# A fused attention and two mixtures on one core: the first unit's ScalarE and VectorE in source order, weight blocks in fixed places, and later token transfers

## The chip, the core and the metric

One NeuronCore of a Trainium2 chip runs the whole kernel as one program. The metric is the device time in microseconds; less is better. TensorE does the matmuls, VectorE, ScalarE and GpSimd the elementwise work, SyncE issues nearly all transfers.

## What is computed

Causal attention over 4 batches, 8 heads, 576 positions, head size 64, with a bias from a running sum of max(s, 0); then two mixtures of 2304 tokens, width 512, inner width 2048.

```
scores = q @ k.T / 8 + min(-(cum[i] - cum[j]), 0), causal;  attn = softmax(scores);  x = attn @ v
x = (h * sigmoid(1.702 h)) @ w_out          with h = x @ w_in        (first mixture)
out = (s * relu(h)**2 + b) @ w_out2         with h = x @ w_in2       (second mixture)
```

The four weight matrices reach the kernel as 64-bit floats. A block of 128 rows or columns is 512 KB.

## The kernel before

**Units.** Attention and first mixture go over eight units: first the first 320 positions of each batch (units 0 to 3), then the other 256 (units 4 to 7). While the mixture of unit u runs on TensorE, the attention of unit u + 1 is put between its matmuls (`run`). Unit 0's attention has no mixture beside it: it runs alone, in ten steps. Step s does the scores (`qk`, three chunks of 64, 128 and 128 rows) of head s, `pv` of head s - 2, and the transposes of head s - 1, in that order on TensorE. Unit 0's matmuls take plain float32 operands; all others take operands split into an upper and a lower part (hi and lo, `split_x`, `split_w`).

**A head on the other engines.** Each chunk's scores are reduced by VectorE (L283) out of one of two PSUM buffers (psS), then ScalarE takes exp (L289). Behind the last chunk VectorE makes tot and its reciprocal (L293, L294), ScalarE normalises the last chunk (L111) and GpSimd the others (L113). ScalarE copies the transposes (L319) and the result of pv (L350). For every second head a token part is split (L390 on ScalarE, L391 on VectorE).

**Weights.** A block is fetched (`fetch_w`, L125), joined from its 64-bit halves (`join_w`: L139 on ScalarE; L140 and L141 on VectorE) and split (`split_w`: the upper part by L149 on ScalarE, the lower by L150 on VectorE). The sixteen blocks of the first layer (wi) are loaded during unit 0's attention, up to two a step from step 1, and wait for their join in tiles with the tag "wo", of which there are sixteen. The sixteen of the second layer (wo) are loaded in `run(0)`, through three tiles tagged "pair".

**Order.** The tile framework plans the order of every engine's instructions by its own costs. Within `manual_schedule(engines=...)` the engines named keep the source's order; instructions from elsewhere can still be put between. Before, the whole kernel names TensorE, unit 0's attention TensorE and SyncE, and the last unit's mixture with the second mixture's first block of tokens TensorE, ScalarE and VectorE.

**The last unit and the second mixture.** `first_whole` runs unit 7's mixture alone: 16 blocks h (12 matmuls each), and from the fifth step on the output of the block four earlier. The second mixture's weights go through nine tiles: `fetch_to`, `join_next`, `split_next`, a join in every step between a block's th (L426) and its g (L430). `second` then runs the second mixture on 512 tokens at a time; its tokens come back from DRAM (`fetch_x`, L538) and are split (`parts_x`, L544 on ScalarE, L545 on GpSimd).

Of the kernel before, what the change touches and what calls it, by code (L numbers as in the profile page):

```python
# [11 lines left out]
F32R = mybir.dt.float32r  # L12
# [26 lines left out]
def f32(ap):  # L39
    return ap.bitcast(F32)  # L40
# [27 lines left out]
def fused_kernel(ctx: ExitStack, tc: tile.TileContext, qkT, vP, s, w1i, w1o, w2i, w2o, s2, b2, out):  # L68
# [59 lines left out]
    def join_w(came):  # L128
# [3 lines left out]
        else:  # L132
# [10 lines left out]
            )  # L143
            return f32(lower)

    def split_w(single, tag, f):

        w = wp.tile([P, 2, CM], F32R, tag=tag, name=f"{tag}{f}")
        nc.scalar.activation(w[:, 0, :], single, AF.Copy)  # L149
        nc.vector.tensor_tensor(w[:, 1, :], single, f32(w[:, 0, :]), ALU.subtract)  # L150
        return w

    def load_w(stage, src, tag, f):
        return split_w(join_w(fetch_w(stage, src, f)), tag, f)
# [2 lines left out]
    with ExitStack() as p1:  # L157
# [15 lines left out]
        def setup():  # L173
# [6 lines left out]
            prep_to(0)  # L180
# [41 lines left out]
        def prep(n):  # L222
            u, h = units[n // H], n % H
            J, nj = u.i1, len(u.keys)
            raw = tile([size["n"] + size["keys"]], "raw")

            r = u.b * H + h
            qc, kc = (slice(0, u.n), slice(u.n, u.n + J)) if u.half == 0 else (slice(J, J + u.n), slice(0, J))
            src = qkT[u.b, h, :, : u.n + J] if u.half == 0 else qkT[u.b, h, :, u.i0 :]
            heads[n] = t = {"x": {}, "qc": qc, "kc": kc}  # L230

            def beside(to):
                nc.sync.dma_start(to[D:R, kc], rows_d[0, r, :, :J])
                nc.sync.dma_start(to[D:R, qc], rows_d[1, r, :, u.i0 : u.i1])

            if n < H:
                nc.sync.dma_start(raw[:D, : u.n + J], src[:D])
                if n > 0:
                    beside(raw)
            else:  # L240
                nc.sync.dma_start(raw[:, : u.n + J], src)
            if h % 2 == 0:
                vraw = tile([size["blocks"], P], "vraw")
                nc.sync.dma_start(vraw[:, :nj, :], vP[u.b, h // 2, :, :nj, :])
                vs[n] = vs[n + 1] = vraw
            if n < H:
                t["parts"] = [(raw, R)]
                return


            hi = tile([size["n"] + size["keys"]], "hi", F32R)
            lo = tile([size["n"] + size["keys"]], "lo", F32R)
            beside(f32(lo))
            scaled(nc.scalar if n < 2 * H else nc.vector, hi[:, : u.n + J], raw[:, : u.n + J])
            nc.sync.dma_start(f32(lo[:D, qc]), f32(hi[:D, qc]))
            nc.vector.tensor_tensor(hi[D:, qc], raw[D:, qc], f32(hi[D:, qc]), ALU.subtract)
            nc.gpsimd.tensor_tensor(lo[:D, kc], raw[:D, kc], f32(hi[:D, kc]), ALU.subtract)  # L257
            t["parts"] = [(lo, R), (hi, P)]
            if h % 2 == 0:
                v = tile([size["blocks"], 4, D], "v", F32R)  # L260
# [5 lines left out]
        def qk(n, c):  # L266
            u, t = units[n // H], heads[n]
            a0, a1 = u.chunks[c]
            w = a1 - a0
# [20 lines left out]
            last = len(u.chunks) - 1  # L290
            if c < last:
                return
            nc.vector.tensor_scalar(out=tot[:, : c + 1], in0=tot[:, : c + 1], scalar1=1e-9, scalar2=None, op0=ALU.add)  # L293
            nc.vector.reciprocal(tot[:, : c + 1], tot[:, : c + 1])  # L294
            for k, (b0, b1) in enumerate(u.chunks):
# [73 lines left out]
        n_prep = [0]  # L369

        def prep_to(n):
            while n_prep[0] <= min(n, limit - 1):
                prep(n_prep[0])
                n_prep[0] += 1

        def attend(item):
# [118 lines left out]

        with tc.tile_pool(name="half0", bufs=1) as pool, tc.manual_schedule(engines={PE}):
            attention_pool(pool, B * H, 0)
            x0 = []
            with tc.manual_schedule(engines={PE, SP}):
                setup()  # L500
                for step in range(H + 2):
                    for item in attention_items(step):
                        if item[2] == H - 1 and item[1] == "pv":
                            x0 += [split_x(0, cc) for cc in range(NC - 1)]
                            for f in range(3):
                                h_begin(0, f, x0)
                        if item[2] < H:
                            attend(item)
                    for f in range(len(wi), min(NF, 2 * step)):
                        wi[f] = load_w((wp, "wo", NF), w1i, "wi", f)  # L510
                    if step == 1:
                        nc.sync.dma_start(s_sb, s2.partition_broadcast(P))
                        nc.sync.dma_start(b_sb, b2.partition_broadcast(P))

            def load_wo(f):
                wo[f] = load_w((pool, "pair", 3), w1o, "wo", f)

            run(0, x0)
            for ui in range(1, B - 1):
                run(ui, [])  # L520


        with tc.tile_pool(name="half1", bufs=1) as pool, tc.manual_schedule(engines={PE}):
            attention_pool(pool, 2 * B * H, 1)
            prep_to(B * H)
            for ui in range(B - 1, len(units) - 1):
                run(ui, [])

# [37 lines left out]
    def first_whole(ui):  # L566
# [2 lines left out]
        py = [psY.tile([P, 512], F32, tag="y", name="py3") for _ in range(NC)]  # L569
        for f in range(NF + LEAD):  # L570
            if f < NF:
                for _ in h_item(ui, f, x, join_next):
                    pass
            else:
                join_next()
# [68 lines left out]
            fetch_to(k + 1 + FETCHED)  # L644

    with tc.manual_schedule(engines={PE}):
        xs = [parts_x(fetch_x(*blocks[0], cc), blocks[0][1]) for cc in range(NC)]
        with tc.manual_schedule(engines={PE, ACT, DVE}):
            fetch_to(FETCHED)
            for f in first_whole(len(units) - 1):  # L650
                split_next()
            later, raws = [], []
            for f in second(*blocks[0], xs, False):
                split_next()
                if f in (NF - 5, NF - 1):
                    later += [parts_x(raw, blocks[1][1]) for raw in raws]
                if f in (NF - 9, NF - 5):
                    raws = [fetch_x(*blocks[1], len(later) + cc) for cc in range(2)]
# [48 lines left out]
```

## Time and profile before

| | |
|---|---|
| time, median of 3 runs | 1061.58 us (1060.53 to 1063.24) |
| profiled execution: time, span | 1062.38 us, 1060.6 us |
| TensorE busy (share of the span) | 1016.2 us (96%) |
| VectorE, ScalarE, GpSimd busy | 647.3 us (61%), 535.9 us (51%), 346.5 us (33%) |
| TensorE's waits from 112 to 600 us, all | 11.6 us, the longest 1.5 us |
| one weight block on VectorE (L140, L141, L150, medians up to 112 us) | 0.43, 0.69, 0.68 us |
| a step of the second mixture (760.61 to 766.04 us) | 5.4 us |
| a split of 512 tokens' columns (L544 on ScalarE, L545 on GpSimd) | 0.63, 1.27 us |

The span is the profiled part of the execution. PE is TensorE, PEld its weight loads, DVE VectorE, ACT ScalarE, POOL GpSimd, SP SyncE. "L141" is line 141 of the kernel before. Matmuls overlap their successors, so a group's time is best read from its start to the next group's start.

### The profile page before, as it was taken

The page shows a single profiled execution, that of the slowest core. Times are in us where ns is not written, and L with a number is a line of the kernel's source. Part 1 is how long each engine was busy: PE and PEld are TensorE (multiplying, and loading weights), DVE is VectorE, ACT ScalarE, POOL GpSimd, SP SyncE. Part 2 cuts the span into 40 slices and gives each one's busy share as a digit, 9 for nine tenths or more (in the row PEclk, how much of TensorE's full clock was granted, in tenths as well). Part 3 has the DMA queues.
Part 4 walks back from the last instruction along what each step waited for, and adds up shares of the span by engine and source line. Part 5 has one row for each costly group of instructions (what it writes and reads, how often), then busy time and mean ns, then how long its engine had stood idle before and what let it go on. Part 6 is the DMA issues. An engine that isn't in the chain of part 4 may idle for free.

```text
span 1060.6 us, 17331 instructions
## 1 busy us (share of the span) xinstructions
PE 1016.2 (96%) x6216; PEld 909.3 (86%) x6216; DVE 647.3 (61%) x1441; ACT 535.9 (51%) x1252; POOL 346.5 (33%) x382
## 2 busy tenths in 40 slices
PE   5988999999999999999999989999999999999998
PEld 3458989999989999999999989888788888888887
DVE  4689877567467788878887579864323323232343
ACT  4788856656536646656656567543322322222222
POOL 1115535335335435445445243112410210111011
PEclk9999999999999999999999999999999999999999
DMA  5665332221042232222221176510300100100010
GB/s 180 195 237 184 124 97 61 62 82 44 8 130 75 63 99 70 83 91 72 87 85 51 38 252 209 178 61 21 109 1 0 65 1 1 45 1 1 1 40 21
DMA packets 39181, 85.51 MB, mean 81 GB/s; under 512 B 5660, under 2 KB 16536, under 8 KB 39096
## 3 DMA queue, kind: packets, MB, share of 16 engines
q1 hardware_dynamic: 38888, 84.27, 25.5%
q8 instruction: 49, 0.80, 0.3%
q14 instruction: 36, 0.29, 0.1%
q10 hardware_dynamic: 208, 0.13, 0.0%
HBM read 70.29 MB, written 10.03 MB: 76 GB/s over the span
## 4 chain that ended last, share of the span: by engine, by line
PE 77%; DVE 10%; DMA 4%; ACT 3%; issue 3%; POOL 1%; SPq 1%; DVEq 0%; ACTq 0%; POOLq 0%
PE py L604 17%; PE ph L554 17%; PE py L444 14%; PE ph L404 13%; PE ps L277 5%; PE pst L315 4%; PE po L342 3%; DVE hi L115 3%; PE py L580 2%; DVE x L283 1%; DMA pair<-w1i 1%; PE po L336 1%; ACT x L289 1%; DVE pair L141 1%; DMA pair<-w1o 1%
## 5 line engine op out<-in xcount | busy, mean ns | idle before, releaser
L404 PE MATMUL ph<-xT,wi 128*128 128x320 f32 (+1 forms) x1536 | 246.6, 305 | 10.9 <-DVE th L426 7.2
L404 PEld LDWEIGHTS ph<-xT,wi 128*128 128x128 f32 x1536 | 217.2, 193 | 12.9 <-DVE th L426 7.8
L444 PE MATMUL py<-g,wo 128*128 128x320 f32 (+1 forms) x1344 | 215.1, 304 | 0.0
L604 PE MATMUL py<-wo,g 128*128 128x512 f32 x864 | 208.2, 390 | 1.9 <-POOL g L563 1.8
L554 PE MATMUL ph<-xT,wi 128*128 128x512 f32 (+1 forms) x960 | 208.4, 368 | 0.0
L554 PEld LDWEIGHTS ph<-xT,wi 128*128 128x128 f32 x960 | 169.0, 188 | 31.0
L604 PEld LDWEIGHTS py<-wo,g 128*128 128x128 f32 x864 | 161.1, 188 | 35.9 <-POOL g L563 2.9
L444 PEld LDWEIGHTS py<-g,wo 128*128 128x128 f32 x1344 | 187.9, 189 | 0.8
L558 DVE TENSOR_TENSOR r<-r 128x512 f32<-128x512 f32 (+1 forms) x80 | 53.1, 664 | 195.7 <-ACT r L557 195.7
L431 POOL TENSOR_TENSOR g<-th,g 128x320 fp32r<-128x320 f32 (+1 forms) x128 | 117.3, 917 | 117.5 <-ACT g L430 117.2
L563 POOL TENSOR_TENSOR g<-r,g 128x512 fp32r<-128x512 f32 (+1 forms) x40 | 48.9, 1222 | 308.6 <-PE py L604 167.5
L289 ACT ACTIVATE x<-x,m 64x64 f32<-64x64 f32 (+2 forms) x160 | 89.5, 560 | 100.1 <-DVE m L283 98.5
L557 ACT ACTIVATE r<-ph 128x512 f32<-128x512 f32 (+1 forms) x80 | 44.4, 555 | 152.0 <-PE ph L554 150.4
L257 POOL TENSOR_TENSOR lo<-raw,hi 64x576 fp32r<-64x576 f32 (+1 forms) x56 | 68.3, 1220 | 122.3 <-issue 57.1
L283 DVE CUSTOM_DVE_ANT_0 x<-ps,mask 64x64 f32<-64x64 f32 (+2 forms) x160 | 68.0, 426 | 52.3 <-PE ps L277 50.5
L315 PE MATMUL pst<-ident,x 128*128 128x128 f32 (+2 forms) x480 | 85.8, 287 | 10.0 <-DVE ph L324 8.1
L562 ACT ACTIVATE g<-r 128x512 fp32r<-128x512 f32 (+1 forms) x80 | 47.1, 589 | 93.0 <-DVE r L559 93.0
L113 POOL TENSOR_SCALAR x<-x,tot 64x64 f32<-64x64 f32 (+1 forms) x96 | 47.6, 503 | 94.1 <-DVE tot L294 66.4
L321 ACT ACTIVATE ph<-pst 64x256 fp32r<-64x256 f32 (+2 forms) x144 | 67.0, 473 | 20.7 <-PE pst L315 19.2
L315 PEld LDWEIGHTS pst<-ident,x 128*128 128x128 f32 (+2 forms) x480 | 54.7, 136 | 24.9 <-DVE ph L324 13.0
L430 ACT ACTIVATE g<-th 128x320 fp32r<-128x320 f32 (+1 forms) x128 | 56.3, 440 | 35.6 <-DVE th L426 35.0
L115 DVE TENSOR_SCALAR hi<-raw 128x832 fp32r<-128x832 f32 (+1 forms) x48 | 69.2, 1441 | 2.3 <-DMA raw<-qkT 2.2
(71 smaller groups left out, 1314.2 us busy)
## 6 DMA issues: line engine op xcount, KB each, us to landing
raw<-qkT SPq DMA_DIRECT2D x32, 416.0 KB
pair<-w1o SPq DMA_DIRECT2D x16, 512.0 KB
pair<-w1i SPq DMA_DIRECT2D x16, 512.0 KB
pair<-w2i SPq DMA_DIRECT2D x16, 512.0 KB
pair<-w2o SPq DMA_DIRECT2D x16, 512.0 KB
raw<-qkT SPq DMA_DIRECT2D x24, 320.0 KB
vraw<-vP SPq DMA_DIRECT2D x16, 320.0 KB
out<-y SPq DMA_DIRECT2D x17, 256.0 KB
```

What stands on the lines that cost most here:

```text
L115: nc.vector.tensor_scalar(out=out, in0=in_, scalar1=scale, scalar2=None, op0=ALU.mult)
L257: nc.gpsimd.tensor_tensor(lo[:D, kc], raw[:D, kc], f32(hi[:D, kc]), ALU.subtract)
L283: nc.vector.tensor_tensor_reduce(out=x[:w, j0:j1], in0=ps[:w, : j1 - j0], in1=mask[:w, WIDE - a0 + j0 : WIDE - a0 + j1], scale=-1.0 / ROOT ...
L289: nc.scalar.activation(x[:w, :a1], x[:w, :a1], AF.Exp, bias=least, scale=-1.0, accum_out=tot[:w, c : c + 1])
L315: nc.tensor.transpose(ps[: j1 - j0, at : at + a1 - a0], t["x"][c][: a1 - a0, j0:j1], ident[: a1 - a0, : a1 - a0])
L321: nc.scalar.activation(t["ph"][:rows, base:end], ps[:rows, :m], AF.Copy)
L404: nc.tensor.matmul(ph[:, :n], wi[f][:, a, cc * P : (cc + 1) * P], x[cc][:, b, :n], start=(k == 0), stop=(k == 3 * NC - 1),)
L430: nc.scalar.activation(g[:, 0, :n], th[:, :n], AF.Copy)
L431: nc.gpsimd.tensor_tensor(g[:, 1, :n], th[:, :n], f32(g[:, 0, :n]), ALU.subtract)
L444: nc.tensor.matmul(py[:, :n], wo[f][:, a, wc], g_t[ui, f][:, b, :n], start=(k == 0), stop=(k == 3 * G - 1))
L554: nc.tensor.matmul(ph[:, :n], wi2[f][:, a, wc], x[cc][:, b, :n], start=(k == 0), stop=(k == 3 * NC - 1))
L604: nc.tensor.matmul(py[t], g2[k][a][:, t * P : (t + 1) * P], wo2[k][:, b, :], start=(k == 0 and i == 0), stop=(k == NF - 1 and i == 2),)
```

## The change

Unit 0's attention now names ScalarE and VectorE too, so that their instructions keep the source's order. Weight work of the first layer has two fixed places (slots) in each step from step 1 on: one in `qk`, between the last chunk's exp and tot, one at the step's end; two more stand in step 8. A slot makes the lower part of the block before it and joins the next one; the upper part is made by GpSimd. Two blocks are fetched in each step from step 0 on, a step ahead of their slots. `prep` is cut in two: the transfers of a head (`prep`) and its hi and lo (`prep_parts`); from the second unit on, a head's raw transfer is issued two heads ahead, its parts one ahead as before. The token splits of unit 0 are put behind the odd heads' pv.

In `first_whole` the first join stands in step 3 in place of step 0. The second mixture's first 512 tokens, which were fetched and split ahead of `first_whole`, are now fetched in its steps 9 and 13 and split in steps 13 and 15. The next 512 are fetched in steps 9 and 13 (before 7 and 11) and split in steps 13 and 15 (before 11 and 15) of `second`.

```diff
-    def split_w(single, tag, f):
+    def upper_w(single, tag, f, engine):
         w = wp.tile([P, 2, CM], F32R, tag=tag, name=f"{tag}{f}")
-        nc.scalar.activation(w[:, 0, :], single, AF.Copy)
+        scaled(engine, w[:, 0, :], single)
+        return w
+
+    def lower_w(single, w):
         nc.vector.tensor_tensor(w[:, 1, :], single, f32(w[:, 0, :]), ALU.subtract)
         return w
...
+            if between is not None:
+                between()
             nc.vector.tensor_scalar(out=tot[:, : c + 1], in0=tot[:, : c + 1], scalar1=1e-9, scalar2=None, op0=ALU.add)
...
-        def prep_to(n):
-            while n_prep[0] <= min(n, limit - 1):
+        n_prep, n_parts = [0], [H]
+
+        def prep_to(n, m):
+
+            while n_prep[0] <= min(max(n, m), limit - 1):
                 prep(n_prep[0])
                 n_prep[0] += 1
+            while n_parts[0] <= min(n, limit - 1):
+                prep_parts(n_parts[0])
+                n_parts[0] += 1
...
-                    prep_to(n + 1)
-                qk(n, k)
+                    prep_to(n if n == H - 1 else n + 1, n + 1 if n < H else n + 2)
+                qk(n, k, between)
...
+            x0, came1, lower1 = [], [], []
+
+            def weights_slot():
+                if lower1:
+                    single, f = lower1.pop()
+                    lower_w(single, wi[f])
+                if len(wi) < len(came1):
+                    f = len(wi)
+                    single = join_w(came1[f])
+                    wi[f] = upper_w(single, "wi", f, nc.gpsimd)
+                    lower1.append((single, f))
+
+            with tc.manual_schedule(engines={PE, SP, ACT, DVE}):
                 setup()
                 for step in range(H + 2):
+                    slot = weights_slot if step > 0 else None
+                    if step == H:
+                        prep_to(H, H + 1)
+                    if step >= H:
+                        weights_slot()
                     for item in attention_items(step):
-                        if item[2] == H - 1 and item[1] == "pv":
-                            x0 += [split_x(0, cc) for cc in range(NC - 1)]
+                        _, kind, n, _ = item
+                        if kind == "pv" and n == H - 1:
                             for f in range(3):
                                 h_begin(0, f, x0)
-                        if item[2] < H:
-                            attend(item)
-                    for f in range(len(wi), min(NF, 2 * step)):
-                        wi[f] = load_w((wp, "wo", NF), w1i, "wi", f)
+                        if n < H:
+                            attend(item, slot)
+                            if kind == "pv" and n % 2 and n < H - 1:
+                                x0.append(split_x(0, n // 2))
+                    if slot:
+                        slot()
+                    for f in range(len(came1), min(NF, 2 * step + 2)):
+                        came1.append(fetch_w((wp, "wo", NF), w1i, f))
...
-                for _ in h_item(ui, f, x, join_next):
+                for _ in h_item(ui, f, x, join_next if f >= 3 else None):
...
-        xs = [parts_x(fetch_x(*blocks[0], cc), blocks[0][1]) for cc in range(NC)]
...
+            def tokens_step(f, t0, n):
+
+                if f in (NF - 3, NF - 1):
+                    later.extend(parts_x(raw, n) for raw in raws)
+                if f in (NF - 7, NF - 3):
+                    raws[:] = [fetch_x(t0, n, len(later) + cc) for cc in range(2)]
```

## Rows read from the trace of the kernel before

**Rows 1.** Windows: stretch, busy us and instructions by engine, clock, DMA, GB/s.
```profile
86.00:112.00 26.00, 22.36 (x155) 20.88 (x155) 25.54 (x57) 23.42 (x60) 15.72 (x19) 1.00 0.58 183
640.00:660.00 20.00, 20.00 (x169) 20.00 (x168) 19.07 (x32) 14.56 (x31) 8.45 (x7) 1.00 0.63 198
```
**Rows 2.** Timeline, TensorE, unit 0's attention: start us, us, instruction, [wait before].
```profile
18.11 2.48 PE L277 MATMUL ps<-raw 68*64 68x64 f32 x6
...
26.65 1.43 PE L277 MATMUL ps<-raw 68*128 68x320 f32 x2 [0.54 <-DVE m L283]
28.01 2.80 PE L336 MATMUL po<-ph,vraw 64*64 64x320 f32 x6
...
32.18 2.48 PE L277 MATMUL ps<-raw 68*64 68x64 f32 x6
...
61.39 2.79 PE L336 MATMUL po<-ph,vraw 64*64 64x320 f32 x6
65.35 1.67 PE L315 MATMUL pst<-ident,x 64*64 64x64 f32 x6 [1.16 <-POOL x L113]
```
**Rows 3.** Timeline, TensorE, from the mixture's first matmuls to 107 us.
```profile
66.67 5.19 PE L404 MATMUL ph<-xT,wi 128*128 128x320 f32 x27
71.79 1.54 PE L336 MATMUL po<-ph,vraw 64*64 64x320 f32 x6
75.47 0.48 PE L404 MATMUL ph<-xT,wi 128*128 128x320 f32 x1 [2.14 <-ACT xT L390]
...
106.35 0.41 PE L277 MATMUL ps<-lo 68*128 68x320 f32 x1 [1.05 <-DVE m L283]
```
**Rows 4.** Timeline, ScalarE and VectorE, unit 0's attention.
```profile
16.77 0.49 DVE L283 CUSTOM_DVE_ANT_0 x<-ps,mask 128x320 f32<-128x320 f32 x1 [0.70 <-PE ps L277]
...
17.91 0.55 ACT L289 ACTIVATE x<-x,m 128x320 f32<-128x320 f32 x1
...
26.38 0.21 DVE L283 CUSTOM_DVE_ANT_0 x<-ps,mask 64x64 f32<-64x64 f32 x1
...
40.59 0.54 ACT L111 ACTIVATE x<-x,tot 128x320 f32<-128x320 f32 x1
41.04 0.79 ACT L319 ACTIVATE ph<-pst 64x320 f32<-64x320 f32 x2
...
53.11 0.69 ACT L139 ACTIVATE pair<-pair 128x512 f32<-128x512 f32 x1 [0.48 <-DMA pair<-w1i]
...
53.83 0.69 DVE L141 SCALAR_TENSOR_TENSOR pair<-pair 128x512 uint32<-128x512 uint32 x1 [0.22 <-ACT pair L139]
...
63.73 1.76 ACT L149 ACTIVATE wo<-pair 128x512 fp32r<-128x512 f32 x3
```
**Rows 5.** Timeline, GpSimd and VectorE, from 59 to 63 us.
```profile
59.00 0.85 POOL L257 TENSOR_TENSOR lo<-raw,hi 64x320 fp32r<-64x320 f32 x1 [2.99 <-ACT hi L111]
59.05 1.15 DVE L256 TENSOR_TENSOR hi<-raw,hi 64x320 fp32r<-64x320 f32 x1
...
62.50 0.49 DVE L256 TENSOR_TENSOR hi<-raw,hi 64x320 fp32r<-64x320 f32 x1 [1.07 <-ACT hi L111]
62.53 0.83 POOL L113 TENSOR_SCALAR v<-vraw 128x384 fp32r<-128x384 f32 x1 [2.68 <-DMA vraw<-vP]
```
**Rows 6.** Timeline, TensorE and ScalarE, the start of the last unit's mixture.
```profile
608.14 5.92 PE L404 MATMUL ph<-xT,wi 128*128 128x256 f32 x48
...
615.95 0.67 ACT L139 ACTIVATE pair<-pair 128x512 f32<-128x512 f32 x1 [0.64 <-DMA pair<-w2i]
...
618.65 2.93 PE L404 MATMUL ph<-xT,wi 128*128 128x256 f32 x12 [4.59 <-DVE th L426]
...
623.00 1.60 PE L404 MATMUL ph<-xT,wi 128*128 128x256 f32 x12
```
**Rows 7.** TensorE's waits from 112 to 600 us: us in total, times, longest.
```profile
PE ps L277 <- DMA lo<-hi: 1.5, 1, 1.5
```
**Rows 8.** Chain that ended last, in order of time: start us, us, what.
```profile
33.64 7.74 DMA pair<-w1i
```

More of the change, by code (lines that the diff above doesn't have):

```diff
@@ L144, in join_w, with split_w @@
             return f32(lower)
-    def split_w(single, tag, f):
+    def upper_w(single, tag, f, engine):
         w = wp.tile([P, 2, CM], F32R, tag=tag, name=f"{tag}{f}")
-        nc.scalar.activation(w[:, 0, :], single, AF.Copy)
+        scaled(engine, w[:, 0, :], single)
+        return w
+    def lower_w(single, w):
         nc.vector.tensor_tensor(w[:, 1, :], single, f32(w[:, 0, :]), ALU.subtract)
         return w
+    def split_w(single, tag, f):
+        return lower_w(single, upper_w(single, tag, f, nc.scalar))
     def load_w(stage, src, tag, f):
@@ L179, in setup @@
             nc.gpsimd.memset(minus, -ROOT)
-            prep_to(0)
+            prep_to(0, 0)
             u, t = units[0], heads[0]
@@ L229, in prep @@
             src = qkT[u.b, h, :, : u.n + J] if u.half == 0 else qkT[u.b, h, :, u.i0 :]
-            heads[n] = t = {"x": {}, "qc": qc, "kc": kc}
+            heads[n] = t = {"x": {}, "qc": qc, "kc": kc, "raw": raw}
             def beside(to):
@@ L234, in beside @@
                 nc.sync.dma_start(to[D:R, qc], rows_d[1, r, :, u.i0 : u.i1])
+            t["beside"] = beside
             if n < H:
@@ L239, in prep @@
                     beside(raw)
+                t["parts"] = [(raw, R)]
             else:
@@ L242, in prep, with prep_parts @@
             if h % 2 == 0:
[L243 to L248, printed above, removed]
+                vs[n] = vs[n + 1] = tile([size["blocks"], P], "vraw")
+                nc.sync.dma_start(vs[n][:, :nj, :], vP[u.b, h // 2, :, :nj, :])
+        def prep_parts(n):
+            u, h, t = units[n // H], n % H, heads[n]
+            J, nj, raw, qc, kc, beside = u.i1, len(u.keys), t["raw"], t["qc"], t["kc"], t["beside"]
             hi = tile([size["n"] + size["keys"]], "hi", F32R)
@@ L259, in prep @@
             if h % 2 == 0:
-                v = tile([size["blocks"], 4, D], "v", F32R)
+                v, vraw = tile([size["blocks"], 4, D], "v", F32R), vs[n]
                 src = vraw[:, :nj].rearrange("p j (a d) -> p j a d", a=2)
@@ L264, in prep, with qk @@
                 vs[n] = vs[n + 1] = v
-        def qk(n, c):
+        def qk(n, c, between=None):
             u, t = units[n // H], heads[n]
@@ L367, in attention_items, with attend @@
             return sorted(items)
-        n_prep = [0]
-        def prep_to(n):
-            while n_prep[0] <= min(n, limit - 1):
+        n_prep, n_parts = [0], [H]
+        def prep_to(n, m):
+            while n_prep[0] <= min(max(n, m), limit - 1):
                 prep(n_prep[0])
                 n_prep[0] += 1
-        def attend(item):
+            while n_parts[0] <= min(n, limit - 1):
+                prep_parts(n_parts[0])
+                n_parts[0] += 1
+        def attend(item, between=None):
             _, kind, n, k = item
@@ L513, in fused_kernel @@
                         nc.sync.dma_start(b_sb, b2.partition_broadcast(P))
+                while len(wi) < NF or lower1:
+                    weights_slot()
+                x0.append(split_x(0, NC - 1))
             def load_wo(f):
@@ L524, in fused_kernel @@
             attention_pool(pool, 2 * B * H, 1)
-            prep_to(B * H)
+            prep_to(B * H, B * H + 1)
             for ui in range(B - 1, len(units) - 1):
@@ L646, in fused_kernel @@
     with tc.manual_schedule(engines={PE}):
-        xs = [parts_x(fetch_x(*blocks[0], cc), blocks[0][1]) for cc in range(NC)]
         with tc.manual_schedule(engines={PE, ACT, DVE}):
+            later, raws = [], []
+            def tokens_step(f, t0, n):
[3 more added lines that the diff above has]
+                    raws[:] = [fetch_x(t0, n, len(later) + cc) for cc in range(2)]
             fetch_to(FETCHED)
@@ L651, in fused_kernel @@
                 split_next()
-            later, raws = [], []
+                tokens_step(f, *blocks[0])
+            xs, later = later, []
             for f in second(*blocks[0], xs, False):
                 split_next()
[L655 to L658, printed above, removed]
+                tokens_step(f, *blocks[1])
         for k, (t0, n) in enumerate(blocks[1:], 1):
```

2 lines of the change are left out of this document (removed).

## The prediction

> **What bounds the kernel now.** I read three views in turn. The windows come first: VectorE is the full engine from 86 to 112 us, 25.54 of 26.00 us, while TensorE has 22.36 [rows 1]. Over the whole span TensorE is busy 96% (table), so only places where it waits can give time back. TensorE's own order of time shows two that this change touches: the first unit's attention with what follows it, up to 106 us [rows 2, 3], and one wait of 4.59 us at 614 us, at the start of the last unit's mixture [rows 6]. Between 112 and 600 us it waits some 12 us in all (table), in pieces of 1.5 us and less. The third view, ScalarE's and VectorE's order of time, says what stood ahead of the instruction waited for [rows 4].
>
> In the first unit a step on TensorE is scores (qk), pv, transposes. From 26.65 the last score chunk takes 1.36 us until pv at 28.01; pv and transposes together 4.17, until 32.18 [rows 2]. A whole qk is 2.48 with its last drain, 2.4 to the next instruction, so a step without waits is 6.6 us. From 18.11 to 61.39 six steps took 43.28 us, 7.21 each [rows 2]: 0.6 us of each is waiting. Then 27 matmuls of the mixture run from 66.67 to 71.79, the last pv ends at 73.33, and TensorE waits 2.14 us for the last token split [rows 3].
>
> **The change, part by part.**
>
> *First unit.* Removed from ScalarE: 16 copies of a weight block (L149). They go to GpSimd, at about 1.1 us each (0.83 us for 384 columns [rows 5], times 512/384); bounds 0.8 and 1.8 (0.66 us of a collision on top, below). Nothing waits for one soon: its VectorE half comes a slot later. The fetch of two blocks moves one step ahead. The rest of the work is the same; what changes is where it stands in ScalarE's and VectorE's queues. That is the cost to work out.
>
> By the source a step is now, on ScalarE: three exps, join a (L139), normalise (L111), copy of pv (L350), in every second step a split (L390), two copies of transposes (L319), join b (L139). On VectorE: three reduces (L283), lower, L140, L141 of join a, tot and reciprocal, lower, L140, L141 of join b; then the next step's first reduce. So that reduce stands behind L141 of join b, which stands behind L139, which stands behind the copy of the step's last transposes. TensorE's third score chunk needs the first chunk's PSUM buffer, that is, this reduce. This closes a loop from step to step: reduce to third chunk 0.27 us (26.38 to 26.65 [rows 2, 4]); third chunk to pv 1.36, pv and transposes 4.17 [rows 2]; their last copy some 0.5 (0.79 for two, the first of which overlaps [rows 4]); L139 to L141 0.72 (53.11 to 53.83 [rows 4]); L141 0.69 [rows 4]. Sum 7.7 us a step. ScalarE's own path round the loop (reduce, exp, L139, L141, tot, L111, L350, copies, L139, L141, each from start to start or to its end) comes to 7.4 to 8.0 us. Before had 7.21.
>
> The loop first bites in step 2. In step 1 the last reduce starts at 16.77 (0.49), exp follows (0.55), then L139 and L141 (0.72 + 0.69), some 0.4 for tot and reciprocal, L111 0.45 (40.59 to 41.04), copies 0.79, L139 and L141 again 1.41 [rows 4]: the first reduce of step 2 comes at 22.3, its third chunk at 22.6. Before, the third chunk of the step that begins at 18.11 was free to start at 19.2 (2.4 - 1.36 = 1.05 behind 18.11). Five more steps of 7.7 bring the third chunk of step 7 to 61.1, and 1.36 + 4.17 later step 8 begins: 66.6, where before had 61.39, 5.2 us later. The tail is better: before waits 1.16 us ahead of the last transposes, at 65.35 [rows 2], and now the last x is ready long before; pv and transposes 4.2 and 0.5 for a copy give 71.3, the 27 matmuls 5.12 more, 76.4, pv 1.54, 77.9 [rows 3], and the split needs only its copy and itself, 0.9 us in place of 2.14, since no weight work is ahead of it. The mixture goes on at 78.8, 3.3 us later than 75.47.
>
> From 75.47 to 106.35, the last wait of this stage [rows 3], before takes 30.9 us, bound by VectorE. Two things are given back there. The second layer's blocks (wo) can take their tiles once the last first-layer block has been fetched: before got its first three at 63.73 [rows 4]. Between 66.6 and 78.8 the new order leaves VectorE two joins, three lower halves and two small subtractions, some 5 of 12.2 us; the other 7 take the lower halves of three wo blocks and about two whole ones. One block costs VectorE 0.43 + 0.69 + 0.68 = 1.8 us (table), so two more blocks done by the time the mixture goes on are 3.6 us less behind it: 3.3 - 3.6 = -0.3. For wo blocks that the planner slips into the loop, and for VectorE instructions held up by GpSimd, I add 1.5 us (bounds 0 and 8, below). First unit: +1.2 us. Its lower bound is -4: no loop at all, six steps at 6.6 in place of 7.2.
>
> *GpSimd beside VectorE.* A VectorE subtract that started beside a GpSimd instruction took 1.15 us, and 0.49 alone [rows 5]: 0.66 us lost. There are 16 new GpSimd copies and two VectorE subtractions of two SBUF inputs per block. In the loop the copy of join b runs beside the reduces and that of join a beside tot, so few collide: 1.5 us. If each of 14 collides once in the loop it is 14 x 0.66 = 9 us, of which the free time of the loop's other path takes a part: 5 to 8.
> The Trainium skill, page "SBUF — State Buffer", section "Who interferes with whom", speaks against moving the copies: a VectorE instruction with two SBUF inputs and a GpSimd instruction that reads SBUF share a read interface, and the second to start is blocked until the first is done. The trace agrees, with the 1.15 against 0.49 us above. By the rule taken for every copy the sum would have the upper figure, 8 us; by my placement it has the lower.
>
> *Fetching raw heads two ahead* (all later units): one wait for a head's operands in all of 112 to 600 us, 1.5 us, and it is for hi's own copy into lo [rows 7], which isn't moved. The raw transfers are hidden behind a whole step. 0 us, bounds -1.5 and +1.5 (that wait gone, or one more).
>
> *Last unit's mixture.* Before, four blocks of 12 matmuls end at 614.06 (608.14 + 5.92). The fifth needs a PSUM buffer that VectorE frees (th), and VectorE stands behind a join whose block arrives only for 615.95; the fifth starts at 618.65, its 12 matmuls take 2.93 us, and the sixth starts at 623.00, behind 12 of the output [rows 6]. Two groups of 12 should take 2.96 us (5.92 / 48 x 24). So 623.00 - 614.06 - 2.96 = 5.98 us are lost. Now the first join comes behind the fourth block, and the token transfers that went ahead of the weights are gone. Even if the block came no earlier than 615.95, the block held up by that join would be the eighth, due at about 622.7. So all 5.98 are won. Late next: token splits, four times 0.63 us of ScalarE and 1.27 us of GpSimd (table), stand at the 14th and 16th blocks, where VectorE is 19.07 of 20.00 busy [rows 1]; that may hold up the second mixture's first VectorE work. The four GpSimd halves are 5 us; VectorE finds some free time in the four short steps, so I take 0.6 of 0 to 2 us. Last unit: -5.4 us.
>
> *Next tokens' transfers and first splits* two steps later in the second mixture: 0 us, hidden by the two steps that stay, 5.4 us each (table); without that cover they would cost the transfer of two 256 KB pieces.
>
> **Sum.** 1.2 - 5.4 = -4.2 us against the profiled execution, 1062.38 (span 1060.6 and 1.8 around it): 1058.2. That execution lies 0.8 above the median of 1061.58; the same step from the median gives 1057.4.
>
> **Rivals.**
> 1. *No loop: the slots are hidden.* For it: ScalarE loses 16 copies of 0.6 us (1.76 for three [rows 4]), 9.4 us. Against: the reduce stands behind join b by the source. First unit -4: 1061.6 - 4 - 5.4 = 1052.2.
> 2. *The port decides.* GpSimd's copies hold VectorE up once per slot, 5 us beyond mine: 1062.4. For it: 1.15 against 0.49 us [rows 5]. Against: in the loop the copies fall beside reduces, which read PSUM and one SBUF tensor.
> 3. *The weights come late (slower).* ScalarE and VectorE now wait for a block at a fixed place. In odd steps SyncE issues its two blocks only behind a V transfer that waits for that step's pv, some 1.5 us before the next step; join a wants one 5 us into it. The chain of waits has a block that took 7.74 us [rows 8]. It decides once landing takes more than 6.5 us (1.5 + 5): then the four steps behind odd ones lose 1.2 us for the first block, and as much for the second. 8 x 1.2 = 10 us: 1068.
> 4. *Nothing won in the last unit:* the wait comes back as the second mixture's: 1063.
>
> **How the numbers follow.** Mine 0.45 (own range 1054 to 1061), rival 1 0.20, rival 2 0.17, rival 3 0.13, rival 4 0.05. 0.3% is 3.2 us, about what a measurement of this kernel can tell from no change. Faster, below 1058.4: 0.35 of mine and all of rival 1, 0.55. Slower, above 1064.8: most of rival 3, a third of rival 2, 0.17. Same: 0.28. The range takes in rival 1 and rival 2 and leaves out the ends of 1 and 3: 1051.5 to 1065.
>
> **What the profile after would show.** Right: in steps 2 to 7 TensorE waits about 1.2 us each for a reduce ahead of the third score chunk; step 8 begins near 66.6; the wait for the last split is under 1 us; at the last unit the 4.59 us are gone, and no wait over 1 us follows up to the second mixture. Wrong: steps of 6.6 us (rival 1), VectorE subtractions over 1 us beside L113 copies (rival 2), L139 or L140 waiting for a block's transfer (rival 3), a wait near 660 to 670 us (rival 4). A planner that orders the stretch from 112 to 600 us otherwise would also make it wrong; 12 us of waits lie there.

## The result and the profile after

The changed kernel takes 1071.91 us (median of 4 runs, 1070.74 to 1073.36) against 1061.51 for the kernel before: ratio 1.0097, 95% interval 1.0079 to 1.0115. It is slower, where I had forecast 1057.4. The profiled span is 1071.6 us, 11.0 more than before.

Three points in the two traces split these 11.0 us. Up to SyncE's first write of the first unit's result to memory (x_d<-y, L455 before and L470 after) 15.12 us are lost: 140.92 before, 156.04 after. From there to the last unit's mixture (608.14 [rows 6], 623.31 after) it is 467.22 and 467.27: nothing. From there to the second mixture 52.30 before (608.14 to 660.44) and 46.08 after, 6.22 won; in the second mixture and to the end 400.16 and 402.21, 2.05 given back. 15.12 + 0.05 - 6.22 + 2.05 = 11.0. The first two lines are SyncE's, before and after, the third is TensorE's before:

```profile
140.92 0.93 SPq L455 DMA_DIRECT2D x_d<-y  x1
...
156.04 0.70 SPq L470 DMA_DIRECT2D x_d<-y  x1
...
660.44 8.35 PE L554 MATMUL ph<-xT,wi 128*128 128x512 f32 x36
```

TensorE's order of time after, first unit (start, length; in brackets the wait ahead of it and for whom); it answers to [rows 2, 3]:

```profile
22.32 1.43 PE L286 MATMUL ps<-raw 68*128 68x320 f32 x2 [2.19 <-DVE m L292]
...
31.45 1.44 PE L286 MATMUL ps<-raw 68*128 68x320 f32 x2 [2.17 <-DVE m L292]
...
39.82 1.44 PE L286 MATMUL ps<-raw 68*128 68x320 f32 x2 [1.42 <-DVE m L292]
...
47.42 0.81 PE L286 MATMUL ps<-raw 68*128 68x320 f32 x2 [1.21 <-DVE m L292]
...
55.16 1.43 PE L286 MATMUL ps<-raw 68*128 68x320 f32 x2 [1.99 <-DVE m L292]
...
62.76 1.43 PE L286 MATMUL ps<-raw 68*128 68x320 f32 x2 [0.65 <-DVE m L292]
...
70.71 2.80 PE L347 MATMUL po<-ph,vraw 64*64 64x320 f32 x6 [2.34 <-ACT ph L330]
...
74.61 4.88 PE L419 MATMUL ph<-xT,wi 128*128 128x320 f32 x27
...
84.92 0.63 PE L419 MATMUL ph<-xT,wi 128*128 128x320 f32 x1 [3.96 <-ACT xT L405]
86.75 1.70 PE L419 MATMUL ph<-xT,wi 128*128 128x320 f32 x5 [1.20 <-DVE xT L406]
```

Each step from step 2 on waits for a reduce (L292) ahead of its third chunk. From one of these third chunks to the next it is 9.13, 8.37, 7.60, 7.74 and 7.60 us. 7.60 is the loop that the prediction had worked out (7.7). The second and the fourth hold a token split, which takes longer (see the run with the slot ahead of the transposes); the fourth is shortened by TensorE's clock, at 47.42 (last section). Then come two waits that the prediction did not have at this size: 2.34 ahead of step 8, and 3.96 plus 1.20 for the last token split. VectorE and ScalarE show what stood ahead:

```profile
27.58 0.47 DVE L140 TENSOR_SCALAR pair<-pair 128x512 uint32<-128x512 uint32 x1 [0.95 <-DMA pair<-w1o]
...
29.63 0.43 DVE L140 TENSOR_SCALAR pair<-pair 128x512 uint32<-128x512 uint32 x1 [0.65 <-DMA pair<-w1o]
29.97 1.29 DVE L141 SCALAR_TENSOR_TENSOR pair<-pair 128x512 uint32<-128x512 uint32 x2
31.17 0.21 DVE L292 CUSTOM_DVE_ANT_0 x<-ps,mask 64x64 f32<-64x64 f32 x1
```

```profile
68.20 1.78 ACT L111 ACTIVATE wo<-pair 128x512 fp32r<-128x512 f32 x3
69.89 0.45 ACT L405 ACTIVATE xT<-xraw 128x320 fp32r<-128x320 f32 x1
70.25 0.78 ACT L330 ACTIVATE ph<-pst 64x320 f32<-64x320 f32 x2
...
83.83 0.68 ACT L111 ACTIVATE wo<-pair 128x512 fp32r<-128x512 f32 x1 [1.62 <-DVE pair L141]
84.40 0.47 ACT L405 ACTIVATE xT<-xraw 128x320 fp32r<-128x320 f32 x1
```

Blocks of the second layer (w1o, wo) are not part of the written order, so the planner put them between its instructions: joins that wait for their transfer ahead of a reduce at 27.58 to 31.17, three upper halves ahead of the copy of the last transposes (L330) at 68.20, another ahead of the last token split at 83.83.

The last unit, TensorE's order of time after; it answers to [rows 6]:

```profile
623.31 7.36 PE L419 MATMUL ph<-xT,wi 128*128 128x256 f32 x60
...
662.19 7.36 PE L619 MATMUL py<-g,wo 128*128 128x256 f32 x60
669.39 8.35 PE L593 MATMUL ph<-xT,wi 128*128 128x512 f32 x36
679.86 4.61 PE L643 MATMUL py<-wo,g 128*128 128x512 f32 x12 [2.12 <-POOL g L602]
```

The 4.59 us wait [rows 6] is gone, and a wait of 2.12 stands at the start of the second mixture. The 12 matmuls behind it take 4.61 us, where the same 12 before took 3.06: the granted clock is 0.56 from 680 to 682 us and 0.64 from there to 684.3. Against these 2.1 and 1.6 us stands a wait of before's second mixture, which is gone after:

```profile
757.75 3.02 PE L604 MATMUL py<-wo,g 128*128 128x512 f32 x12 [1.56 <-POOL g L563]
```

With what the matmuls ahead of it drain, that is 1.7 us back, and 2.1 + 1.6 - 1.7 is the 2.05 given back, to within 0.1.

### The profile page after: what moved, and what is told of

It is laid out like the page before. It is cut to its first block, busy times and chain, and to the rows that moved or that the text cites. A ratio compares the mean times of both kernels' runs of the same rounds, so it can differ in the third digit from the quotient of the medians.

```text
span 1071.6 us, 17352 instructions
## 1 busy us (share of the span) xinstructions
PE 1016.8 (95%) x6216; PEld 909.3 (85%) x6216; DVE 653.5 (61%) x1441; ACT 528.2 (49%) x1236; POOL 356.7 (33%) x398
## 4 chain that ended last, share of the span: by engine, by line
PE 77%; DVE 11%; DMA 4%; ACT 4%; issue 2%; SPq 1%; DVEq 0%; ACTq 0%
PE py L643 19%; PE ph L593 18%; PE py L459 13%; PE ph L419 13%; PE pst L326 4%; PE ps L286 4%; DVE hi L115 3%; PE po L353 3%; DMA pair<-w1o 3%; PE py L619 2%; DVE x L292 1%; DMA raw<-qkT 1%; PE po L347 1%; DVE pair L141 1%; ACT x L298 1%
## 5 line engine op out<-in xcount | busy, mean ns | idle before, releaser
L292 DVE CUSTOM_DVE_ANT_0 x<-ps,mask 64x64 f32<-64x64 f32 (+2 forms) x160 | 67.6, 426 | 55.8 <-PE ps L286 54.3
L440 ACT ACTIVATE th<-ph 128x320 f32<-128x320 f32 (+1 forms) x128 | 51.6, 403 | 45.4 <-PE ph L419 41.8
L441 DVE SCALAR_TENSOR_TENSOR th<-th,ph 128x320 f32<-128x320 f32 (+1 forms) x128 | 57.5, 450 | 22.8 <-ACT th L440 21.8
```

Of the source, the lines that this page charges most:

```text
L292: nc.vector.tensor_tensor_reduce(out=x[:w, j0:j1], in0=ps[:w, : j1 - j0], in1=mask[:w, WIDE - a0 + j0 : WIDE - a0 + j1], scale=-1.0 / ROOT ...
L441: nc.vector.scalar_tensor_tensor(out=th[:, :n], in0=th[:, :n], scalar=1.0, in1=ph[:, :n], op0=ALU.add, op1=ALU.mult)
```

## The experiments

My theory: the first unit is slow because work that TensorE waits for now stands behind weight work on ScalarE and VectorE, by the written order and by what the planner puts between. Rivals: GpSimd's copies hold VectorE up; the blocks come late from memory; VectorE's amount of work sets the stage after the attention, whatever the steps take.

The table has a ratio to before (95% interval) and two points of each profiled run: when the mixture goes on behind its last wait for ScalarE's half of the last token split (xT), and when the first unit's first result leaves; the stage is the time between. One profiled run can lie 3 us from its kernel's median (two tiles: 1056.4, median 1059.7), so the points of two kernels are compared as two runs, not as two medians.

| kernel | median us | ratio | mixture goes on | result leaves | stage |
|---|---|---|---|---|---|
| before | 1061.5 | | 75.47 | 140.92 | 65.45 |
| after | 1071.9 | 1.0097 (1.0079-1.0115) | 84.92 | 156.04 | 71.12 |
| second mixture alone | 1056.7 | 0.9962 (0.9947-0.9976) | 75.16 | 140.78 | 65.62 |
| planner's order | 1065.6 | 1.0037 (1.0023-1.0051) | 79.06 | 147.31 | 68.25 |
| copies on ScalarE | 1073.4 | 1.0119 (1.0104-1.0134) | 87.29 | 157.66 | 70.37 |
| slot ahead of transposes | 1070.7 | 1.0084 (1.0066-1.0102) | 83.72 | 153.56 | 69.84 |
| second layer behind | 1066.4 | 1.0047 (1.0032-1.0063) | 76.75 | 148.43 | 71.68 |
| three edits of order | 1067.2 | 1.0049 (1.0032-1.0066) | 76.23 | 147.99 | 71.76 |
| planner, copies on ScalarE | 1062.1 | 1.0004 (0.9989-1.0019) | 75.42 | 145.80 | 70.38 |
| raw heads two ahead alone | 1061.4 | 0.9996 (0.9980-1.0013) | 75.73 | 145.22 | 69.49 |
| blocks a step earlier alone | 1061.1 | 0.9996 (0.9981-1.0010) | 75.40 | 144.41 | 69.01 |
| two tiles for w1o | 1059.7 | 0.9993 (0.9980-1.0006) | 73.49 | 140.85 | 67.36 |
| two joins moved | 1055.2 | 0.9930 (0.9908-0.9952) | 76.70 | 142.16 | 65.46 |
| two joins moved, again | 1052.6 | 0.9920 (0.9905-0.9935) | 73.84 | 139.15 | 65.31 |

**Second mixture alone.** The kernel before with the last hunks of the diff only:

```
-                for _ in h_item(ui, f, x, join_next):
+                for _ in h_item(ui, f, x, join_next if f >= 3 else None):
...
+                tokens_step(f, *blocks[0])
```

> The kernel before with only the second-mixture part of the change. If the last unit's part is worth what the trace after shows, the 6.2 us won between the last unit's first h and the second mixture less the 2.1 us given back behind it, the time is 1061.5 - 4.2 = 1057.3. My forecast's term gives 1056.1. If the gain in that place needs the rest of the change, there is none: 1061.5. If the rest of the change is what costs the 2.1 us, 1055.3.

1056.7, 4 us won. By its trace 6.2 us are won up to the second mixture (654.28 for 660.44) and 0.5 given back in it, and the clock does not fall behind the wait of 2.14 that stands there here too. The rest of the change then costs 1071.9 - 1056.7 = 15.2 us; between the two traces 15.3 us lie ahead of the first unit's first result.

**Planner's order.** After, with the first unit's section as before:

```
-            with tc.manual_schedule(engines={PE, SP, ACT, DVE}):
+            with tc.manual_schedule(engines={PE, SP}):
```

> The changed kernel, but ScalarE and VectorE of the first unit are ordered by the planner again (TensorE and SyncE stay in source order); slots, GpSimd copies and fetches as changed. If the order on the two engines costs the first unit its 15.2 us, they come back, and the last unit's 4.2 stay won: 1053 to 1059. If GpSimd's copies beside VectorE are the cost (rival 2), or the places of the fetches (rival 3), most of the 15 us stay: 1068 to 1072.

1065.6, between the two expectations. The written order costs 6.3 us by the medians, not 15; the other 8.9 stay with slots, copies and fetches.

**Copies on ScalarE.** After, with the 16 upper halves given to ScalarE in their places:

```
-                    wi[f] = upper_w(single, "wi", f, nc.gpsimd)
+                    wi[f] = upper_w(single, "wi", f, nc.scalar)
```

> The changed kernel with the 16 weight copies on ScalarE again, in the same places. If GpSimd beside VectorE is the cost, 5 to 9 us come back: 1063 to 1067. If the order is the cost, a copy of 0.66 us more stands in ScalarE's chain in each slot, of which the wait for tot hides about half: five steps by 0.3 to 0.6, 1073 to 1075.

1073.4, 1.4 more than after, with intervals that overlap: GpSimd beside VectorE is not what slows the changed kernel.

**Slot ahead of the transposes.** After, the second weight slot directly behind a step's pv:

```
+                        if kind == "pv" and slot:
+                            slot()
-                    if slot:
+                    if slot and step < 2:
                         slot()
```

> The changed kernel with the second weight slot of a step behind its pv, ahead of its transposes, in place of behind the step's last copy. If the chain from the reduce over the last copy, L139 and L141 to the next step's reduce sets the step, the step falls from 7.7 us to 6.6 to 7.2, step 8 begins 2.5 to 5 us earlier, and the time is 1067 to 1069.5. If VectorE's total work up to 122 us sets the end of this stage whatever the steps take, 1071 to 1073. If GpSimd is the cost, no change: 1071.9.

1070.7, 1.2 less and within the noise, a miss: step 8 begins at 69.04 in place of 70.71. The kernel with three edits of order, below, has the same slots without the planner's blocks between, and shows why. Its TensorE and, beside the step at 48.76, its ScalarE and VectorE:

```profile
41.71 2.94 PE L286 MATMUL ps<-raw 68*64 68x64 f32 x6
...
48.76 1.41 PE L286 MATMUL ps<-raw 68*64 68x64 f32 x4
51.59 1.44 PE L286 MATMUL ps<-raw 68*128 68x320 f32 x2 [1.42 <-DVE m L292]
...
57.13 2.40 PE L286 MATMUL ps<-raw 68*64 68x64 f32 x5
```

```profile
47.62 0.56 ACT L111 ACTIVATE x<-x,tot 128x320 f32<-128x320 f32 x1 [1.11 <-DVE tot L305]
48.21 0.43 ACT L361 ACTIVATE xraw<-po 64x320 f32<-64x320 f32 x1
48.67 0.47 ACT L405 ACTIVATE xT<-xraw 128x320 fp32r<-128x320 f32 x1
49.05 0.66 ACT L139 ACTIVATE pair<-pair 128x512 f32<-128x512 f32 x1
```

```profile
49.17 0.49 DVE L406 TENSOR_TENSOR xT<-xraw,xT 128x320 fp32r<-128x320 f32 x1 [1.65 <-ACT xT L405]
49.58 0.69 DVE L153 TENSOR_TENSOR wi<-pair,wi 128x512 fp32r<-128x512 f32 x1
50.19 0.42 DVE L140 TENSOR_SCALAR pair<-pair 128x512 uint32<-128x512 uint32 x1
50.71 0.69 DVE L141 SCALAR_TENSOR_TENSOR pair<-pair 128x512 uint32<-128x512 uint32 x1
51.32 0.21 DVE L292 CUSTOM_DVE_ANT_0 x<-ps,mask 64x64 f32<-64x64 f32 x1
```

The steps are now 7.05 and 8.37 us in turn. The kernel with the second layer behind (next run), which differs by this edit and by the place of the last split, has 7.60 without a split (20.54 to 28.14, and 52.01 to 59.60) and the same 8.37 with one:

```profile
43.64 1.44 PE L286 MATMUL ps<-raw 68*128 68x320 f32 x2 [0.65 <-DVE m L292]
...
52.01 1.44 PE L286 MATMUL ps<-raw 68*128 68x320 f32 x2 [1.41 <-DVE m L292]
```

So the link over the last copy sets the steps without a split, and the edit wins 0.55 us in each of these. A step with a split closes on ScalarE: normalise, copy of pv, split, then VectorE's half of the split and its three instructions of the slot, and only then the reduce. There the edit changes nothing.

**Second layer behind.** After, with the first three second-layer blocks fetched in the written order and joined and split behind the last token split:

```
                 x0.append(split_x(0, NC - 1))
+                for f in range(3):
+                    wo[f] = split_w(join_w(first3[f]), "wo", f)
```

> The changed kernel, but the first three second-layer blocks are joined and split behind the last token split, so that the planner can put none of them into the first unit's attention. If these blocks cost what the trace after shows (2.0 us in the fourth step, a 2.3 us wait for a copy ahead of step 8, most of the 4.0 us wait for the last split), step 8 begins near 66.5, the mixture goes on near 77, and the time is 1063 to 1067. If VectorE's total work sets the end of this stage, the blocks are missing afterwards, three by 1.8 us: 1070 to 1076.

1066.4, 5.5 us less. Step 8 begins at 65.26 and the mixture goes on at 76.75, 8.2 us earlier than after. 1.8 of these stand ahead of step 2's third chunk (20.54 for 22.32), and there the kernel before has an early second-layer block too (L140 at 7.41, after at 7.21); the other 6.4 are, but for some 0.5 us of a higher clock in one step (36.51 to 43.64, 7.13 us), what the planner had put between from there on. But the stage behind it is not shorter, 71.68 us.

**Three edits of order.** The same, with the slot ahead of the transposes, and the last token split directly behind its pv:

```
-                            if kind == "pv" and n % 2 and n < H - 1:
+                            if kind == "pv" and n % 2:
                                 x0.append(split_x(0, n // 2))
...
-                x0.append(split_x(0, NC - 1))
```

> The changed kernel with three edits to its order: the second weight slot ahead of the transposes, the last token split directly behind its pv, the first three second-layer blocks behind both. If order is the whole loss, the first unit is as long as before or shorter and the last unit's 4.2 stay won: 1055 to 1060. If VectorE's work behind it sets the end, 1066 to 1072.

1067.2, no better. The mixture goes on at 76.23, 0.8 later than before; the result leaves 7.1 later. The windows from that point on show the difference between this kernel and after. Before, after, and this one, each over nearly the same matmuls (columns: window, length, busy time and instructions of TensorE, weight loads, VectorE, ScalarE, GpSimd, then granted clock, DMA share, GB/s):

```profile
75.50:121.00 45.50, 41.52 (x266) 39.21 (x267) 44.69 (x105) 40.52 (x100) 22.73 (x27) 0.92 0.53 167
```

```profile
84.90:136.00 51.10, 43.27 (x266) 40.86 (x267) 40.09 (x101) 38.19 (x97) 21.16 (x27) 0.89 0.45 142
```

```profile
76.20:128.00 51.80, 44.06 (x274) 41.97 (x275) 49.38 (x111) 42.38 (x105) 21.90 (x27) 0.90 0.56 172
```

With three blocks of some 1.8 us fewer done ahead of it, VectorE of this kernel is full (49.38 of 51.80 us) and has 4.7 us more to do than before: here its amount of work sets the stage, as the third rival has it. After has the opposite: it has its lead, 4.6 us less to do than before, and takes 5.6 us longer, because VectorE stands idle for 11.0 of 51.1 us where before had 0.8. TensorE's clock is not the cause: its matmuls take 1.75 us more after (43.27 for 41.52, granted clock 0.89 for 0.92), but they take 42.84 at 0.89 in the second-mixture part alone too, from 75.2 to 120.7 us, and its stage is 65.62.

**Planner, copies on ScalarE.** Both edits at once:

```
-            with tc.manual_schedule(engines={PE, SP, ACT, DVE}):
+            with tc.manual_schedule(engines={PE, SP}):
...
-                    wi[f] = upper_w(single, "wi", f, nc.gpsimd)
+                    wi[f] = upper_w(single, "wi", f, nc.scalar)
```

> The planner's order on ScalarE and VectorE, as in the run that gave 1065.6, with the 16 weight copies on ScalarE again as well. What is left of the first unit's part are the places of the slots and the earlier fetches. If GpSimd's copies cost the 8.9 us that lie between that run and the second-mixture part alone (by holding up VectorE or GpSimd's own normalising copies), they come back: 1057 to 1060. If the places and fetches cost them: 1064 to 1067.

1062.1: by the planner's order GpSimd's copies cost 3.5 us, and 5.4 remain. Its step 7 begins earlier than before's (52.62, before 54.30), step 8 and the mixture at the same time; the stage is 4.9 us longer.

**Raw heads two ahead alone; blocks a step earlier alone.** Each is added to the second-mixture part: the split of prep into prep and prep_parts with its calls, and in the other kernel the earlier loads:

```
-                    prep_to(n + 1)
+                    prep_to(n if n == H - 1 else n + 1, n + 1 if n < H else n + 2)
```

```
-                    for f in range(len(wi), min(NF, 2 * step)):
+                    for f in range(len(wi), min(NF, 2 * step + 2)):
```

> The kernel before with the second-mixture part, and beside it only the raw heads fetched two ahead (the first unit's weights, splits and order as before). My forecast has 0 for it, 1.5 us either way: 1055 to 1058. If it is this part that holds up the 5 us which the planner's order with ScalarE's copies still lacked against the second-mixture part alone, 1060 to 1063.

> The kernel before with the second-mixture part, and beside it only the first layer's weight blocks loaded one step earlier. If earlier blocks let the planner put second-layer work further ahead of what TensorE waits for, 1059 to 1063; if the fetch's place is free, 1055.5 to 1058.

1061.4 and 1061.1: each takes back the whole gain, some 4.5 us; the run before, which has both and the slots' places as well, lost 5.4, so they do not add. By the traces 4.4 and 3.6 us are lost up to the first unit's first result, nearly all of it in the same stage (69.5 and 69.0 us). 1.5 and 1.8 more are lost in the second mixture, whose code is the same: there TensorE's clock falls behind the 2.1 us wait as it does after (12 matmuls take 4.36 and 4.61 us, in the second-mixture part alone 3.02). In the first of the two kernels:

```profile
88.76 2.72 DVE L153 TENSOR_TENSOR wo<-pair,wo 128x512 fp32r<-128x512 f32 x1
91.40 0.21 DVE L292 CUSTOM_DVE_ANT_0 x<-ps,mask 64x64 f32<-64x64 f32 x1
```

```profile
88.56 0.71 POOL L113 TENSOR_SCALAR x<-x,tot 64x64 f32<-64x64 f32 x2 [1.20 <-DVE tot L305]
89.24 1.68 POOL L446 TENSOR_TENSOR g<-th,g 128x320 fp32r<-128x320 f32 x2
```

```profile
91.67 0.42 PE L286 MATMUL ps<-lo 68*128 68x320 f32 x1 [1.80 <-DVE m L292]
```

The planner has put the lower half of a second-layer block ahead of a reduce, that half falls beside four GpSimd instructions and takes 2.72 us in place of 0.69, and TensorE waits 1.80. In the second-mixture part alone the third chunks of this stage wait for no reduce.

**Two tiles for w1o.** The second-mixture part, with two tiles in place of three for the blocks on their way, to see whether the supply sets this stage: VectorE waits for it 4.1 us in after's window, and in before's no such wait is listed.

```
-                wo[f] = load_w((pool, "pair", 3), w1o, "wo", f)
+                wo[f] = load_w((pool, "pair", 2), w1o, "wo", f)
```

> The kernel before with the second-mixture part, and two tiles in place of three for the second layer's blocks on their way from memory. If the supply of these blocks is what the stage from 75 to 121 us lives on (VectorE waits 0.1 us for them before, 1.6 to 4.1 in the kernels whose stage is 4 to 6 us longer), VectorE's waits for their transfer grow to 5 us and more, the stage grows by as much, and the time is 1061 to 1066. If VectorE's amount of work alone sets the stage, or if its order does, the time stays within 2 us: 1055 to 1059.

1059.7, 3 us more than with three tiles, between the two expectations. The time alone settles nothing, and the profiled run is the fastest of ten, 1056.4. In it VectorE waits 3.7 us for w1o and the stage is only 67.36. With the kernel of three edits, whose VectorE waits 0.6 us for w1o in a stage of 71.76, that speaks against the supply as the cause, but does not exclude it as a part.

**Two joins moved.** The second-mixture part; the last two weight blocks of the last unit are joined and split at two later steps:

```
-            else:
+            elif f < NF + LEAD - 2:
                 join_next()
...
             for f in second(*blocks[0], xs, False):
                 split_next()
+                if f in (4, 6):
+                    join_next()
+                    split_next()
```

> The kernel before with the second-mixture part alone, and in it the last two weight blocks of the last unit are joined and split two steps into the second mixture instead. If the 2.1 us wait at the start of the second mixture is VectorE's queue of blocks (two by 1.8 us), it goes: 1056.7 - 2.1 = 1054.6. If it is GpSimd's or the last unit's sums' own time, nothing changes: 1056.7. If the two blocks are then late in the second mixture: 1057 to 1060.

> The kernel that ran at 0.9930 of before, timed on the same chip as the run beside it: the last two blocks of the last unit joined and split inside the second mixture. By its trace the second mixture takes 398.4 us in place of 400.6, so 2.1 us less than the second-mixture part alone: ratio 0.994. If the gap between the two was of the first unit's own scatter, 0.996.

Ratios 0.9930 and 0.9920, the fastest kernel here. TensorE of the second-mixture part alone and of this one at the start of the second mixture:

```profile
654.28 8.35 PE L554 MATMUL ph<-xT,wi 128*128 128x512 f32 x36
664.77 3.02 PE L604 MATMUL py<-wo,g 128*128 128x512 f32 x12 [2.14 <-POOL g L563]
```

```profile
652.39 8.35 PE L554 MATMUL ph<-xT,wi 128*128 128x512 f32 x36
660.58 2.88 PE L604 MATMUL py<-wo,g 128*128 128x512 f32 x12
```

So the wait of 2.1 us is VectorE's queue of weight blocks ahead of the first g, as the runs show, and not the token splits, which are the same in both. Against the second-mixture part the ratios fell by 3.4 and 4.5 us, more than the wait. Of the eleven profiled kernels with a wait there five have the fall of the clock behind it, some 1.5 us; that its absence is part of the gain is possible and not shown.

## Why the prediction was wrong

**The step that failed** is "so two more blocks done by the time the mixture goes on are 3.6 us less behind it". I took VectorE's busy time of the stage for its length, because before it was full there [rows 1]. The lead was there: 40.09 us of work against 44.69. But VectorE takes its work in the planner's order, and in the stage as it came out it waits: 4.1 us for w1o, 2.2 for score chunks, the rest in pieces for ScalarE and GpSimd. The stage took 71.12 us in place of 65.45: 5.7 lost where I had 3.6 won and 1.5 of trouble, 7.8 us off.

**The second** is "the split needs only its copy and itself, 0.9 us in place of 2.14, since no weight work is ahead of it". It had the planner's second-layer blocks ahead of it. I did count them as filling VectorE's free time there, but at no cost. The third chunk of step 7 came at 62.76 for 61.1, 1.7 us late: against 7.7 the step with the blocks cost 1.4, the first one with a split 0.7, and an earlier start and the other steps gave 0.4 back. 2.3 came ahead of step 8 and 2.0 behind its start, where the split came 14.2 us later for 12.2: 6.1 us in all (84.92 for 78.8). With these blocks put behind, the mixture goes on at 76.75. 6.1 + 7.8 = 13.9, which is the first unit's 15.1 less the forecast 1.2. My bound of 8 us for the planner's blocks and the port together held the first of these, not both.

**The loop** was right for a step without a split: 7.60 us for 7.7, third chunk of step 2 at 22.32 for 22.6. A step with a split takes 8.37, by ScalarE's path; the prediction had that path at 7.4 to 8.0, because its list leaves out the split and VectorE's half of it.

**GpSimd beside VectorE** (rival 2) is not the cause: in the written order the copies save 1.4 us against ScalarE's, within the noise, in the planner's they cost 3.5. The 0.49 us that the prediction calls alone was not alone: a GpSimd instruction began 0.03 us after it [rows 5]. What the rows show is that the subtract which began second took 1.15 us, and the one which began first 0.49.

**Raw heads two ahead** was right for the units it serves, 467.2 us in both, and wrong as a whole: "0 us, bounds -1.5 and +1.5" left out that the planner orders the first unit's last stage anew. I had named that for 112 to 600 us; it came at 75 to 140.

**The last unit** was right in its mechanism: 6.22 us won for 5.98. What was late next was mis-sized: a wait of 2.12 for 0.6, and by VectorE's weight blocks, not by the splits. Two things that the prediction did not have nearly cancel: the lower clock behind that wait, 1.6 us, and the wait at 757.75 that before had, 1.7. It gave the next tokens' transfers and splits 0; that wait stood for a g of GpSimd (755.99) which came behind token splits of GpSimd (L545), and it is gone in every kernel here with the second-mixture part.

**Rival 3**, the slower side, had the right sign but another mechanism: the first layer's blocks are never waited for at a fixed place; it is the second layer's, which have no place.

**What stays open.** Undone in turn, the written order, the GpSimd copies and what else the first unit has of the change account for the 15.2 us (6.3, 3.5 and 5.4), but these depend on each other. The stage is 68 to 72 us in each kernel with an edit to the first unit's order, copies or fetches, and 65.3 to 65.6 in those without (67.4 with two tiles). It is long in two ways: with VectorE full and more to do (three edits) and with VectorE waiting (after). That the planner's order is the cause of the second is argued from a few rows (a block ahead of a reduce, waits for w1o); no run kept the stage's order and changed the rest.

## What to carry to other kernels

An order written for some instructions of an engine does not keep others out: list what else may be put on that engine, and ask of each whether something that TensorE waits for can come to stand behind it. A lead of an in-order engine is worth its time only where the engine had no waits; busy time of a stage is a lower bound of its length. Where a planner orders the neighbourhood, test each harmless edit alone: two that should have cost nothing cost 4.5 us each, and a kernel with both did not cost 9.

## What the runs showed of the hardware

The granted clock of the windows and the durations did not agree in the first unit's attention. After, three windows and TensorE in them and ahead of them:

```profile
37.00:46.00 9.00, 7.58 (x23) 3.76 (x22) 6.20 (x17) 5.60 (x16) 2.71 (x4) 1.00 0.87 281
46.00:52.00 6.00, 4.79 (x18) 2.45 (x16) 3.49 (x12) 3.40 (x10) 1.83 (x5) 0.73 0.13 35
52.00:61.00 9.00, 7.01 (x20) 3.33 (x19) 5.97 (x17) 5.46 (x16) 2.62 (x5) 0.50 0.87 298
```

```profile
36.99 1.42 PE L286 MATMUL ps<-raw 68*64 68x64 f32 x4
...
45.36 0.85 PE L286 MATMUL ps<-raw 68*64 68x64 f32 x4
...
51.76 1.41 PE L286 MATMUL ps<-raw 68*64 68x64 f32 x4
```

The same four matmuls take 1.42 us at 36.99, where the row of 37 to 46 us says 1.00, and 1.41 at 51.76, where it says 0.50 (the lower of the two levels, 1.2 GHz); only at 45.36 are they 0.85. Before, too, the third chunk takes 1.43 us [rows 2] in a stretch that says 1.00, as after at 55.16 where it says 0.50; at 47.42 it is 0.81. So the 1.00 ahead of 45 us is not borne out by the durations. At the start of the second mixture row and durations agree: 4.61 us for 12 matmuls at 0.56 and 0.64, 3.06 at 1.00. The wait at that place was followed by the lower level in five profiled runs and not in six others, with the same code there; no run explains why.

The 2.72 us of a VectorE subtract of two SBUF inputs beside four GpSimd instructions, where 0.69 is usual, is the longest such hold-up seen here. The Trainium skill, page "SBUF — State Buffer", section "Who interferes with whom", has VectorE's second SBUF input come through a read interface that GpSimd shares, under an exclusive lock. The trace agrees that the two were not served at once, and shows more: the subtract, listed from 88.76, ended at 91.48, behind not one of GpSimd's instructions but all four (88.56 to 90.92), and 0.56 us more.
